# Attention and two mixture layers: K loaded in runs of 16s, a new order in the first columns, GpSimd sums in pieces

## The chip, the cores and the metric

The kernel runs on one core of one Trainium2 chip. The metric is the device time of one execution in microseconds (us). The kernel before has a median of 943.73 us over 3 runs (943.45 to 946.13).

## The reference

Three stages follow each other; all inputs are float32. The attention's queries are 8 batches x 8 heads x 576 rows x 64; K and V are averaged over 8 neighbouring rows first, so that each head has 72 keys.

```
k_p = k.reshape(B, H, Sp, pool, D).mean(axis=3)      # B,H,S,D = 8,8,576,64, pool = 8
v_p = v.reshape(B, H, Sp, pool, D).mean(axis=3)
scores = scale * np.matmul(q, k_p.transpose(0, 1, 3, 2))
attn = np.exp(scores - scores.max(-1)); attn /= attn.sum(-1) + 1e-09
x = np.matmul(attn, v_p)                              # then 4608 tokens x 512
# layer 1: e_idx = argmax(x @ w_gate + modality_bias[modality_id])
out[mask] = gate_w[mask, None] * (np.maximum(x[mask] @ w1[e], 0) @ w2[e])   # 8 experts, 512->1024->512
# layer 2: the same with its own weights for rows with x @ w_skip > 0; x is added, other rows stay x
```

## The kernel before

**Columns.** The attention works on 36 columns (c = 0 to 35) of 128 query rows, in a loop that runs three further turns (`LAG`), since the product with V lies three columns behind. In a column TensorE (PE) computes the scores S (L310, eight heads, keys from `KB`), transposes the queries of the column after next (qT, L289), transposes the exponentials of the column before (eT, L357), subtracts the row maxima from the scores (L336, "the exp matmul"; ScalarE's exponential follows it) and multiplies with V (AV, L377, for the column three back). VectorE (DVE) reduces the scores to their maxima `mx` (L316): the exp matmul waits for it. Each of these has few buffers: one PSUM tile for S, and one, `ps_m`, that everything occasional shares (transposed K and V, V times the gating weights, the counts R of the routing).

**K and V.** K and V come in as rows of 8 x 64 numbers (512 a row), and their sums over 8 are made on GpSimd (POOL) as a tree of three additions (L181, L182, L183), or on DVE as one reduction (L176). Batches 0 and 1 of K are loaded by batch (`kb`, `load_kb`, 126 rows at a time); batches 2 to 7 as four tiles of 108 rows (`kt`, `load_k`), each in two halves of four heads, one DMA a head. `prep_kb` and `prep_k` (L217 to L239) then transpose the sums on PE, `prep_v1` (L255) and `prep_v2` (L274) do it for V. The tables `pool_at` and `prep_at` say behind which column each of these stands.

**Loads.** All loads are issued by SyncE (SP) in one queue, in the order of `order` and as `next_kv` and `next_q` are called; eight DMA semaphores go round, so that SP's next issue waits for the one eight before.

**Routing beside the columns.** The first mixture layer needs every token's expert. Its work is cut into small steps of generators, of which `bg.tick()` takes the next; some five ticks fall in a column, twice as many from c = 22 (`bg.pace`). `route` (9 columns a call, started at c = 12, 21 and 30) takes the maximum of the gating values `LG` (`rt_mx`), marks the expert by three small GpSimd instructions (`rt_eq`, L840 to L844), reduces the marks (`rt_my`, L850, on DVE), makes a running count over the nine columns (a scan on DVE, L867, and the carry L871), ranks by two matmuls R (L882, L883), and leaves the position `BB`. `lag` gives the number of ticks between its steps. `route_places` then makes 18 tiles `OB` of 128x128 on GpSimd (L911), from which, after c = 30, a matmul W (L1031) and a gather fetch the first blocks of tokens. `count` makes a further R (L923) of the counts. In c = 32 and 33 `ps_x` transposes tokens of the first block, whose low half `xl` DVE writes (L320).

**After the attention** come the two layers in blocks of 256 tokens, where each float32 product is three matmuls. The change touches none of this.

Of the kernel before, what the change touches and what calls it, by code (L numbers as in the profile page):

```python
# [14 lines left out]
ALU = mybir.AluOpType  # L15
# [19 lines left out]


NB0 = 2
KT = (B - NB0) * SP // 4
TILES = [(NB0 * SP + KT * i, NB0 * SP + KT * i + KT) for i in range(4)]

KR = [(126 * i, min(126 * i + 126, H * SP)) for i in range(5)]
VC = 96
# [13 lines left out]
def attention(tc, g, q, k, v, mid, w_gate, bias, const, moe):  # L56
# [3 lines left out]
    nc = tc.nc  # L60
    with ExitStack() as ctx:
# [28 lines left out]
        cols = []  # L90
# [11 lines left out]
        raw_t = {}  # L102
# [5 lines left out]
        def load_kb(b, i0, i1):  # L108

            if ("kb", b) not in raw_t:  # L110
                raw_t["kb", b] = raw.tile([128, 5, POOL * D], F32, tag="k", name="kb", bufs=3)
            a = raw_t["kb", b]
            n = KR[i0][1] - KR[i0][0]
            for i in range(i0, i1):
                nc.sync.dma_start(out=a[0:n, i:i + 1, :], in_=rows(k, b, *KR[i], 1))

        def load_k(t, hf):
            a = raw.tile([128, 5, POOL * D], F32, tag="k", name="kt", bufs=3)[:, 0:4]
            for b, s0, s1, p0 in segments(t):
                for h in range(4):  # L120
                    nc.sync.dma_start(
                        out=a[p0:p0 + s1 - s0, h, :],
                        in_=k[b, 4 * hf + h, s0 * POOL:s1 * POOL, :].rearrange(
                            "(s r) d -> s (r d)", r=POOL),
                    )
# [58 lines left out]

        def sums_of(key, shape):
# [7 lines left out]
            pool_rows(d[0:n, i0:i1, :], raw_t["kb", b][0:n, i0:i1, :], eng)  # L193

        def pool_k(t, hf, eng):
            d = sums_of(("k", t), [KT, H, D])
            pool_rows(d[:, 4 * hf:4 * hf + 4, :], raw_t.pop(("k", t, hf))[0:KT], eng)

        def pool_v(b, hf, eng, i0=0, i1=3):
            d = sums_of(("v", b), [VC, 6, D])  # L200
# [222 lines left out]
        def idle():  # L423
            for _ in range(3):
# [2 lines left out]
        av_t = {}  # L427

        P, V = nc.gpsimd, nc.vector
        pool_at = {0: [(pool_kb, 1, 2, 4, P), (pool_kb, 1, 0, 2, V), (pool_kb, 1, 4, 5, V)],  # L430
                   1: [(pool_v, 1, 0, P)]}
# [5 lines left out]
        for b, cs in ((1, (3, 4, 4)), (2, (5, 6, 7)), (3, (10, 11, 12)), (4, (14, 15, 16)),  # L437
                      (5, (18, 19, 20)), (6, (20, 21, 22)), (7, (24, 25, 26))):
            for i, c in enumerate(cs):
                pool_at.setdefault(c, []).append((pool_v, b, 1, V, i, i + 1))  # L440
        prep_at = {1: [(prep_v1, 0)], 2: [(prep_kb, 1), (prep_v2, 0)],
                   5: [(prep_v1, 1)], 6: [(prep_v2, 1)], 7: [(prep_k, 0)],
                   8: [(prep_v1, 2, P)], 9: [(prep_v2, 2)], 11: [(prep_k, 1)],
                   13: [(prep_v1, 3, P)], 14: [(prep_v2, 3)],
                   17: [(prep_v1, 4)], 18: [(prep_v2, 4)], 20: [(prep_k, 2)],
                   21: [(prep_v1, 5)], 22: [(prep_v2, 5)], 24: [(prep_v1, 6)], 25: [(prep_k, 3)],
                   26: [(prep_v2, 6)], 28: [(prep_v1, 7)], 29: [(prep_v2, 7)]}

        def free_after(key):
# [110 lines left out]

        route_at = {12: (0, 9), 21: (9, 9), 30: (18, 9)}
        for c in range(NC + LAG):
            if c < NC:
                next_q(cols[c][0] + (5 if c > 1 else 4))
                next_kv(c)
                next_q(cols[c][0] + 5)
            bg.pace = {22: 2, 32: 1, 34: 2, 36: 3}.get(c, bg.pace)
            if 4 <= c < NC - 1:
                emit_S(c, lambda: emit_qT(c + 2))
            elif c < 4:  # L570
# [255 lines left out]
def route(tc, g, r, lg, mask, c0, n, sp, pp, eng, wait=1, then=(), lag=(0, 0)):  # L826
# [30 lines left out]
    if n > 2:  # L857
# [322 lines left out]
class Moe:  # L1180
# [307 lines left out]
    def prepare_first(self, c, sm, ps_q, ps_m, late):  # L1488
# [607 lines left out]
```

## Time and profile before

| | us |
|---|---|
| median of 3 runs | 943.73 |
| the profiled execution | 941.72 |
| its span in the trace | 940.0 |
| PE busy | 891.0 |
| DVE busy | 705.2 |
| GpSimd busy | 513.3 |
| ScalarE busy | 367.7 |

Busy times are of the whole span. The clock that TensorE was granted is on average 0.985 of full speed. The attention, to which the change belongs, ends a little after 200 us. A row of the timeline gives the start, the duration, the engine, the line, the operation, output and inputs, a count where equal instructions were merged, and in brackets the idle time of the engine before it and what released it.

### The profile page before, as it was taken

To read this page: it belongs to the slowest core of one execution; us is meant where nothing else is said; L and a number is where in the kernel's file an instruction comes from. 1 tells how busy PE (TensorE), PEld (TensorE's weight loads), DVE (VectorE), ACT (ScalarE), POOL (GpSimd) and SP (SyncE) were. 2 spreads that over 40 slices of the span, in tenths; PEclk is the share of its full clock that TensorE was granted. 3 is DMA by queue.
4 is the path that set the end of the run, shared out by engine and by line. 5 is a ranking of instruction groups with operands and counts; after the bars stand their busy time and mean duration, and the time that the engine had idled before them with its cause. 6 is when DMAs were issued, how large, how long until landed. Compare 5 with 4: busy or idle time off the path is not lost. (4 is left out here: it accounts for less than half of the span.)

```text
span 940.0 us, 19065 instructions
## 1 busy us (share of the span) xinstructions
PE 891.0 (95%) x6231; PEld 800.9 (85%) x6231; DVE 705.2 (75%) x1815; ACT 367.7 (39%) x727; POOL 513.3 (55%) x763
## 2 busy tenths in 40 slices
PE   8899989899999999998999979999989999999995
PEld 6799879888899999987999869999878988979993
DVE  5477786787778888889877898877565777688663
ACT  3466555453222222251222422213413556565551
POOL 6766696312246657665766557575554343445441
PEclk9899999999999999999999999999999999999999
DMA  9998975523212211431224421227114673671351
GB/s 235 222 254 250 263 206 157 185 70 113 69 65 86 74 41 55 152 144 66 85 81 135 167 79 64 75 81 246 62 61 149 207 236 128 202 246 37 111 161 44
DMA packets 86141, 126.07 MB, mean 134 GB/s; under 512 B 13192, under 2 KB 50104, under 8 KB 85866
## 3 DMA queue, kind: packets, MB, share of 16 engines
q1 hardware_dynamic: 75386, 96.68, 33.1%
q0 software_dynamic: 10608, 27.67, 9.7%
q8 instruction: 63, 1.03, 0.5%
q14 instruction: 84, 0.69, 0.2%
HBM read 182.09 MB, written 39.50 MB: 236 GB/s over the span
## 5 line engine op out<-in xcount | busy, mean ns | idle before, releaser
L1413 PE MATMUL ps_g<-xh,w1h 128*128 128x256 f32 x896 | 255.6, 285 | 3.9 <-DVE hl L1418 2.2
L1413 PE MATMUL ps_g<-xl,w1h 128*128 128x256 f32 x896 | 252.8, 282 | 2.2 <-DVE xl L1366 2.2
L1413 PE MATMUL ps_g<-xh,w1l 128*128 128x256 f32 x896 | 252.0, 281 | 0.0
L1743 DVE CUSTOM_DVE_ANT_0 hr<-x,W 128x512 bf16<-128x512 f32 x324 | 228.2, 704 | 19.1 <-DVEq L1342 6.3
L1462 PE MATMUL ps_g<-w2h,hh 128*128 128x512 f32 x464 | 189.8, 409 | 2.8 <-ACT w2h L1353 1.4
L1462 PE MATMUL ps_g<-w2h,hl 128*128 128x512 f32 x464 | 184.9, 399 | 7.2 <-DVE hl L1418 7.0
L1462 PE MATMUL ps_g<-w2l,hh 128*128 128x512 f32 x464 | 183.6, 396 | 0.0
L1413 PEld LDWEIGHTS ps_g<-xh,w1h 128*128 128x128 f32 x896 | 169.0, 189 | 9.0 <-DVE hl L1418 2.6
L1413 PEld LDWEIGHTS ps_g<-xl,w1h 128*128 128x128 f32 x896 | 168.4, 188 | 3.9 <-DVE xl L1366 3.0
L1413 PEld LDWEIGHTS ps_g<-xh,w1l 128*128 128x128 f32 x896 | 168.8, 188 | 0.0
L1417 ACT ACTIVATE hh<-ps_g 128x512 fp32r<-128x512 f32 (+1 forms) x116 | 67.6, 583 | 246.9 <-PE ps_g L1413 244.7
L1418 DVE SCALAR_TENSOR_TENSOR hl<-ps_g,hh 128x512 fp32r<-128x512 f32 (+1 forms) x116 | 77.5, 668 | 62.6 <-ACT hh L1417 39.0
L911 POOL TENSOR_SCALAR OB<-iota,BB,pay 128x128 bf16<-128x128 bf16 x126 | 110.8, 887 | 22.5 <-DVE BB L899 22.4
L1462 PEld LDWEIGHTS ps_g<-w2h,hl 128*128 128x128 f32 x464 | 87.6, 189 | 30.4 <-DVE hl L1418 8.7
L1462 PEld LDWEIGHTS ps_g<-w2h,hh 128*128 128x128 f32 x464 | 88.0, 190 | 22.2 <-issue 3.7
L1462 PEld LDWEIGHTS ps_g<-w2l,hh 128*128 128x128 f32 x464 | 88.1, 190 | 16.7
L1354 DVE TENSOR_TENSOR w2l<-w2r,w2h 128x512 fp32r<-128x512 f32 x112 | 75.3, 710 | 7.1 <-ACT w2h L1353 4.3
L1333 POOL TENSOR_TENSOR w1l<-w1r,w1h 128x512 fp32r<-128x512 f32 x36 | 46.6, 1314 | 60.6 <-ACT w1h L1330 60.4
L1709 POOL DMA_INDIRECT out_dram<-x,dsi x38 | 47.3, 1244 | 43.5 <-DMA out_dram<-x,dsi 14.8
L1353 ACT CAST w2h<-w2r 128x512 fp32r<-128x512 f32 x112 | 63.9, 617 | 1.4 <-ACTq L1973 1.4
L1330 ACT CAST w1h<-w1r 128x512 fp32r<-128x512 f32 x112 | 63.7, 620 | 0.5 <-ACT hh L1417 0.5
L1323 POOL DMA_INDIRECT xg<-xd,gidx x38 | 44.3, 1165 | 33.6 <-DVE rs_lo L1174 16.5
(298 smaller groups left out, 1403.9 us busy)
## 6 DMA issues: line engine op xcount, KB each, us to landing
w1r<-in_moe_w_dram SPq DMA_DIRECT2D x128, 512.0 KB
w2r<-in_moe_w_dram SPq DMA_DIRECT2D x124, 512.0 KB
x2s<-x SPq DMA_DIRECT2D x19, 522.0 KB
v<-in_v_dram SPq DMA_DIRECT2D x48, 192.0 KB
xd<-x SPq DMA_DIRECT2D x16, 520.0 KB
q_sb<-in_q_dram SPq DMA_DIRECT2D x16, 512.0 KB
kt<-in_k_dram SPq DMA_DIRECT2D x32, 144.0 KB
x2s<-OBx SPq DMA_DIRECT2D x16, 261.0 KB
```

The costliest lines, as they stand in the source:

```text
L911: e.tensor_scalar(g.ob(c)[:, i, :], g.iota, r.BB[:, c:c + 1], r.pay[:, i, c:c + 1], ALU.is_equal, ALU.mult)
L1323: self.nc.gpsimd.indirect_dma_start(out=self.xg[i % 2][:, t, 0:w], out_offset=None, in_=src, in_offset=bass.IndirectOffsetOnAxis(ap=gidx[: ...
L1330: self.nc.scalar.copy(self.w1h[f], raw)
L1333: low() if late is None else late.append(low)
L1353: self.nc.scalar.copy(self.w2h[f], raw)
L1354: (eng or self.nc.vector).tensor_tensor(self.w2l[f], raw, self.w2h[f].bitcast(F32), ALU.subtract)
L1413: nc.tensor.matmul(out, lhsT=a[f][:, k, :], rhs=b[:, k, :], start=(n == 0), stop=(n == 11))
L1417: nc.scalar.activation(out=hh, in_=whole, func=ACTF.Relu)
L1418: nc.vector.scalar_tensor_tensor(hl, in0=whole, scalar=0.0, in1=hh.bitcast(F32), op0=ALU.max, op1=ALU.subtract)
L1462: nc.tensor.matmul(ps, lhsT=a[f][:, tt], rhs=b[f], start=(n == 0), stop=(n == 23))
L1709: self.nc.gpsimd.indirect_dma_start(out=self.out, out_offset=bass.IndirectOffsetOnAxis(ap=self.dsi[i % 2][:, t:t + 1], axis=0), in_=self.x ...
L1743: self.nc.vector.tensor_tensor_reduce(out=self.junk, in0=self.x2[i % 2][:, t, 0:DM], in1=self.W9[:, e, :], scale=1.0, scalar=0.0, op0=ALU. ...
```

## The change

**K loads.** The four tiles of K have 120, 96, 120 and 96 rows in place of 108 each. A DMA takes four heads at once and its rows are a multiple of 16, with what is left over (8 rows) in a DMA of its own. The loads of batches 0 and 1 take 128, 128, 128, 128 and 80 rows (126 and 72 before; the surplus rows are not used).

**Pieces.** GpSimd's first additions are made one row group at a time (256 results each), the second two groups at a time; the third is as before. A half of a K tile has 7 instructions in place of 3, a half of V 6 in place of 3.

**First columns.** `prep_kb(1)` moves from the end of c = 2 to c = 3, behind the exp matmul of that column, so that column 3 stands ahead of it; `prep_v2(0)` moves ahead of the exp matmul of c = 2. Queries are split after that exponential, and the fifth reduction of the second K is one column later. Query loads are issued sooner than K and V.

**Later columns.** The V sums and preparations of batch 2 are a column later, and so is `prep_k(3)`, which now stands inside c = 26. In the routing the lags are other, the carry of the first two calls is made on GpSimd, one copy of the counts moves to ScalarE, the pace of the ticks changes a column earlier at the end, and a flag `bg.shut` holds the second R of `count` back until c = 35.

```
+KG = [NB0 * SP + n for n in (0, 120, 216, 336, 432)]
+TILES = [(KG[i], KG[i + 1]) for i in range(4)]
 def load_kb:
+                n = -(-(KR[i][1] - KR[i][0]) // 16) * 16
+                nc.sync.dma_start(out=a[0:n, i, :], in_=flat[r0:r0 + n])
 def load_k:
-                for h in range(4):
-                    nc.sync.dma_start(out=a[p0:p0 + s1 - s0, h, :], ...
+                cut = s0 + (s1 - s0) // 16 * 16
+                for x0, x1 in ((s0, cut), (cut, s1)):
+                    if x0 < x1:
+                        nc.sync.dma_start(out=a[p0 + x0 - s0:p0 + x1 - s0],
+                            in_=k[b, 4 * hf:4 * hf + 4, x0 * POOL:x1 * POOL, :].rearrange(
+                                "h (s r) d -> s h (r d)", r=POOL))
 def pool_rows:
-                eng.tensor_tensor(t1, a[:, :, 0:4 * D], a[:, :, 4 * D:], ALU.add)
-                eng.tensor_tensor(t2, t1[:, :, 0:2 * D], t1[:, :, 2 * D:], ALU.add)
+                for i in range(m):
+                    eng.tensor_tensor(t1[:, i], a[:, i, 0:4 * D], a[:, i, 4 * D:], ALU.add)
+                for i in range(0, m, 2):
+                    x = slice(i, min(i + 2, m))
+                    eng.tensor_tensor(t2[:, x], t1[:, x, 0:2 * D], t1[:, x, 2 * D:], ALU.add)
 the column loop:
+            if c == 0:
+                for n in (4, 5, 6):
+                    next_q(n)
+                    next_kv(0, 1)
+                next_kv(0)
...
+            elif c < NC:
+                next_q(cols[c][0] + (5 if c < 2 else 6))
+                next_kv(c)
-            bg.pace = {22: 2, 32: 1, 34: 2, 36: 3}.get(c, bg.pace)
+            bg.pace = {22: 2, 31: 1, 33: 2, 36: 3}.get(c, bg.pace)
+            elif c == 2:
+                emit_S(c)
+                emit_eT(c - 1)
+                prep_v2(0)
+                emit_exp(c)
+                split_q(2)
+            elif c == 3:
+                emit_S(c)
+                emit_eT(c - 1)
+                emit_qT(4)
+                emit_exp(c)
+                prep_kb(1)
+            if c == 26:
+                prep_k(3)
             emit_AV(c - LAG)
+            if c == 3:
+                emit_qT(5)
-        (nc.gpsimd, (5, 8) if c0 == 0 else (4, 12))
+        (nc.gpsimd, (5, 1) if c0 == 0 else (6, 3))
 def route:
-        V.tensor_copy(r.carry, I[:, :, n - 1])
+        eng.tensor_copy(r.carry, I[:, :, n - 1])
 def count:
-    nc.vector.tensor_copy(cb, r.carry)
+    (nc.scalar.copy if copy else nc.vector.tensor_copy)(cb, r.carry)
+    while g.bg.shut:
+        yield
 def prepare_first, at c = 32 and 33:
+            self.g.bg.shut = True
```

**The first columns on PE.** Before, from the transposed queries of column 4 (`ps_q`) to the scores of column 4 (the `ps_s<-KB_129` in the last row), with the rest of the nine `ps_k` instructions of the second K left out:

```order
L289 MATMUL ps_q<-ident,qs 128x128 x4
L217 MATMUL ps_k<-ident,kb 64x126
...
L222 MATMUL ps_k<-ident,kb 64x72
L274 MATMUL ps_g<-WGV,vt 96x32 x3
L310 MATMUL ps_s<-KB_128,qt 128x144 x4
L357 MATMUL ps_et<-ident,ec 96x128 x6
L336 MATMUL ps_s<-mx,nident 128x288 x2
L289 MATMUL ps_q<-ident,qs 128x128 x4
L377 MATMUL ps_av<-VB_134,et 128x146 x6
L310 MATMUL ps_s<-KB_129,qt 128x144 x4
```

The same place now, from V times the gating weights (`ps_g`) to the scores of column 4:

```order
L282 MATMUL ps_g<-WGV,vt 96x32 x3
L344 MATMUL ps_s<-mx,nident 128x288 x2
L318 MATMUL ps_s<-KB_128,qt 128x144 x4
L365 MATMUL ps_et<-ident,ec 96x128 x6
L297 MATMUL ps_q<-ident,qs 128x128 x4
L344 MATMUL ps_s<-mx,nident 128x288 x2
L225 MATMUL ps_k<-ident,kb 64x126
...
L230 MATMUL ps_k<-ident,kb 64x72
L385 MATMUL ps_av<-VB_134,et 128x146 x6
L297 MATMUL ps_q<-ident,qs 128x128 x4
L318 MATMUL ps_s<-KB_129,qt 128x144 x4
```

The scores of column 3 (`KB_128`), their exp matmul and `ps_g` stand ahead of the second K's transposes now.

**GpSimd between c = 16 and c = 23.** Before, from the end of the second half of the third K tile, with the 18 tiles `OB` and two halves of V between it and the marks `rt_eq` of the second routing:

```order
L183 TENSOR_TENSOR k<-t_1466 108x256
L911 TENSOR_SCALAR OB<-iota,BB_664,pay_666 128x128 x2
L181 TENSOR_TENSOR t_1536<-v 96x768
L182 TENSOR_TENSOR t_1537<-t_1536 96x384
L183 TENSOR_TENSOR v<-t_1537 96x192
L911 TENSOR_SCALAR OB<-iota,BB_664,pay_666 128x128 x8
L181 TENSOR_TENSOR t_1673<-v 96x768
L182 TENSOR_TENSOR t_1674<-t_1673 96x384
L183 TENSOR_TENSOR v<-t_1674 96x192
L911 TENSOR_SCALAR OB<-iota,BB_664,pay_666 128x128 x8
L840 TENSOR_TENSOR rt_eq<-LG,rt_mx 128x72
```

Now, from the end of the first half of that tile; the two halves of V follow as before behind the last row here, in pieces, with eight and three `OB` behind them, and then `rt_eq`:

```order
L191 TENSOR_TENSOR k<-t_1408 120x256
L944 TENSOR_SCALAR OB<-iota,BB_663,pay_665 128x128 x3
L187 TENSOR_TENSOR t_1479<-kt 120x256 x4
L190 TENSOR_TENSOR t_1480<-t_1479 120x256 x2
L191 TENSOR_TENSOR k<-t_1480 120x256
L944 TENSOR_SCALAR OB<-iota,BB_663,pay_665 128x128 x4
L187 TENSOR_TENSOR t_1551<-v 96x256 x3
```

The first `OB` stands a half of a K tile earlier, so that this half now lies between the first `OB` and `rt_eq`.

**DVE in c = 22 and 23.** Before, from the V scaling `VB` of c = 22 to the reduced marks `rt_my` of c = 23 (each `mx` begins a column):

```order
L316 TENSOR_REDUCE mx<-ps_s 128x8
L260 TENSOR_TENSOR VB_139<-v,half 96x12x64
L176 TENSOR_REDUCE v<-v 96x64
L406 TENSOR_REDUCE LG<-lg 128x8
L838 TENSOR_REDUCE rt_mx<-LG 128x9
L395 TENSOR_SCALAR rec<-ps_av 128x8
L397 RECIPROCAL rec<-rec 128x8
L399 TENSOR_TENSOR lg<-ps_av,rec 128x64
L402 TENSOR_TENSOR x<-ps_av,rec 128x512
L316 TENSOR_REDUCE mx<-ps_s 128x8
L276 TENSOR_TENSOR VB_139<-ps_g,half 96x12x8
L176 TENSOR_REDUCE v<-v 96x64
```

(the next row there is `rt_my`). Now, the end of c = 22 and the `mx` of c = 23:

```order
L181 TENSOR_REDUCE v<-v 96x64
L871 TENSOR_REDUCE rt_mx<-LG 128x9
L414 TENSOR_REDUCE LG<-lg 128x8
L883 TENSOR_REDUCE rt_my<-rt_eq 128x9
L403 TENSOR_SCALAR rec<-ps_av 128x8
L405 RECIPROCAL rec<-rec 128x8
L407 TENSOR_TENSOR lg<-ps_av,rec 128x64
L410 TENSOR_TENSOR x<-ps_av,rec 128x512
L324 TENSOR_REDUCE mx<-ps_s 128x8
```

`rt_my` stands one column earlier, two rows behind `rt_mx`, and ahead of the `mx` of column 23.

## Rows read from the trace of the kernel before

**Rows 1.** The page: busy time and share of the span of each engine.
```profile
PE 891.0 (95%) x6231; PEld 800.9 (85%) x6231; DVE 705.2 (75%) x1815; ACT 367.7 (39%) x727; POOL 513.3 (55%) x763
```

**Rows 2.** Windows: length, busy us (instructions) of each engine, clock, DMA share, GB/s.
```profile
20.00:30.00 10.00, 6.61 (x40) 4.40 (x37) 3.75 (x4) 5.08 (x9) 8.92 (x11) 0.88 1.03 242
30.00:40.00 10.00, 9.16 (x60) 8.72 (x61) 3.42 (x8) 3.77 (x10) 5.58 (x6) 0.78 0.85 220
...
100.00:110.00 10.00, 10.00 (x76) 9.98 (x75) 6.79 (x20) 5.57 (x12) 4.96 (x6) 0.86 1.09 302
...
180.00:190.00 10.00, 9.28 (x70) 8.93 (x71) 5.60 (x20) 4.15 (x12) 3.88 (x6) 0.83 0.49 186
```

**Rows 3.** Timeline of PE in columns 1 to 4.
```profile
20.90 0.39 PE L255 MATMUL ps_v<-ident,v 96*128 96x96 f32 x2 [0.58 <-POOL v L183]
...
23.79 0.51 PE L336 MATMUL ps_s<-mx,nident 128*128 128x288 f32 x2 [0.84 <-DVE mx L316]
25.74 0.66 PE L289 MATMUL ps_q<-ident,qs 128*128 128x128 f32 x4 [1.44 <-ACT qs L167]
...
30.84 1.17 PE L274 MATMUL ps_g<-WGV,vt 128*96 128x32 f32 x6 [1.37 <-ACT KB L231]
31.82 2.27 PE L310 MATMUL ps_s<-KB,qt 128*128 128x144 f32 x8
...
37.23 1.15 PE L310 MATMUL ps_s<-KB,qt 128*128 128x144 f32 x8
```

**Rows 4.** Timeline of ACT: the split of the queries of columns 4 and 5.
```profile
24.64 1.04 ACT L167 COPY qs<-q_sb 128x1024 f32<-128x1024 f32 x1 [3.69 <-DMA q_sb<-in_q_dram]
```

**Rows 5.** Timeline of POOL: the first addition of the first K tile, batch 2.
```profile
34.91 2.35 POOL L181 TENSOR_TENSOR t<-kt 108x1024 f32<-108x1024 f32 x1 [4.11 <-DMA kt<-in_k_dram]
```

**Rows 6.** Timeline of PE: the transposes of that K tile, before S(8).
```profile
54.49 0.53 PE L239 MATMUL ps_k<-ident,k 108*128 108x108 f32 x4
```

**Rows 7.** Timeline of PE: the later waits, c = 17 to 34.
```profile
97.79 0.51 PE L336 MATMUL ps_s<-mx,nident 128*128 128x288 f32 x2 [1.92 <-DVE mx L316]
...
130.21 0.51 PE L336 MATMUL ps_s<-mx,nident 128*128 128x288 f32 x2 [1.15 <-DVE mx L316]
...
135.46 0.51 PE L336 MATMUL ps_s<-mx,nident 128*128 128x288 f32 x2 [0.84 <-DVE mx L316]
...
139.28 0.40 PE L239 MATMUL ps_k<-ident,k 108*128 108x108 f32 x2 [1.62 <-POOL k L183]
...
162.62 1.04 PE L1031 MATMUL W<-er_oa,OB 128*128 128x2 bf16 x36
...
170.82 0.51 PE L336 MATMUL ps_s<-mx,nident 128*128 128x288 f32 x2 [0.98 <-DVE mx L316]
...
180.72 0.18 PE L923 MATMUL R<-rc_cb,ones 128*128 128x8 bf16 x1 [2.19 <-DVE xl L320]
```

**Rows 8.** Timeline of DVE: two scans, the reduced marks, the low half of `ps_x`.
```profile
92.33 2.37 DVE L867 TENSOR_TENSOR_SCAN rt_i<-within,rt_ms 128x72 bf16<-128x72 f32 x1
...
127.91 0.23 DVE L850 TENSOR_REDUCE rt_my<-rt_eq 128x9 f32<-128x72 f32 x1 [1.86 <-POOL rt_eq L844]
...
168.43 0.31 DVE L867 TENSOR_TENSOR_SCAN rt_i<-within,rt_ms 128x72 bf16<-128x72 f32 x1
...
175.57 0.68 DVE L320 TENSOR_TENSOR xl<-ps_x,xh 128x512 fp32r<-128x512 f32 x1
```

**Rows 9.** GpSimd's additions of K by form, 0 to 170 us.
```profile
L181 POOL TENSOR_TENSOR t<-kt 108x1024 f32<-108x1024 f32 x8 | 18.9, 2357 | 4.3 <-DMA kt<-in_k_dram 4.1
...
L183 POOL TENSOR_TENSOR k<-t 108x256 f32<-108x256 f32 x8 | 5.9, 741 | 0.6
```

**Rows 10.** Timeline of POOL: from the first `OB` to the marks, and a K half.
```profile
104.89 1.59 POOL L911 TENSOR_SCALAR OB<-iota,BB,pay 128x128 bf16<-128x128 bf16 x2 [8.20 <-DVE BB L899]
...
126.66 0.30 POOL L840 TENSOR_TENSOR rt_eq<-LG,rt_mx 128x72 f32<-128x72 f32 x1
...
136.54 1.87 POOL L182 TENSOR_TENSOR t<-t 108x512 f32<-108x512 f32 x1
```

More of the change, by code (lines that the diff above doesn't have):

```diff
@@ L37 @@
 NB0 = 2
-KT = (B - NB0) * SP // 4
-TILES = [(NB0 * SP + KT * i, NB0 * SP + KT * i + KT) for i in range(4)]
+KG = [NB0 * SP + n for n in (0, 120, 216, 336, 432)]
+TILES = [(KG[i], KG[i + 1]) for i in range(4)]
+KN = [KG[i + 1] - KG[i] for i in range(4)]
 KR = [(126 * i, min(126 * i + 126, H * SP)) for i in range(5)]
@@ L112, in load_kb @@
             a = raw_t["kb", b]
-            n = KR[i0][1] - KR[i0][0]
+            flat = k.rearrange("b h (s r) d -> (b h s) (r d)", r=POOL)
             for i in range(i0, i1):
-                nc.sync.dma_start(out=a[0:n, i:i + 1, :], in_=rows(k, b, *KR[i], 1))
+                n = -(-(KR[i][1] - KR[i][0]) // 16) * 16
+                r0 = b * H * SP + KR[i][0]
+                nc.sync.dma_start(out=a[0:n, i, :], in_=flat[r0:r0 + n])
         def load_k(t, hf):
@@ L119, in load_k @@
             for b, s0, s1, p0 in segments(t):
-                for h in range(4):
[L121 to L125, printed above, removed]
+                cut = s0 + (s1 - s0) // 16 * 16
+                for x0, x1 in ((s0, cut), (cut, s1)):
+                    if x0 < x1:
+                        nc.sync.dma_start(
+                            out=a[p0 + x0 - s0:p0 + x1 - s0],
+                            in_=k[b, 4 * hf:4 * hf + 4, x0 * POOL:x1 * POOL, :].rearrange(
+                                "h (s r) d -> s h (r d)", r=POOL),
+                        )
             raw_t["k", t, hf] = a
@@ L195, in pool_k @@
         def pool_k(t, hf, eng):
-            d = sums_of(("k", t), [KT, H, D])
-            pool_rows(d[:, 4 * hf:4 * hf + 4, :], raw_t.pop(("k", t, hf))[0:KT], eng)
+            d = sums_of(("k", t), [128, H, D])[0:KN[t]]
+            pool_rows(d[:, 4 * hf:4 * hf + 4, :], raw_t.pop(("k", t, hf))[0:KN[t]], eng)
         def pool_v(b, hf, eng, i0=0, i1=3):
@@ L234, in prep_k @@
             bg.settle()
-            n = KT
-            ks = sum_t.pop(("k", t))
+            n = KN[t]
+            ks = sum_t.pop(("k", t))[0:n]
             ps = ps_m.tile([128, 4, 128], F32, tag="m", name="ps_k")
@@ L429, in attention @@
         P, V = nc.gpsimd, nc.vector
-        pool_at = {0: [(pool_kb, 1, 2, 4, P), (pool_kb, 1, 0, 2, V), (pool_kb, 1, 4, 5, V)],
-                   1: [(pool_v, 1, 0, P)]}
+        pool_at = {0: [(pool_kb, 1, 2, 4, P), (pool_kb, 1, 0, 2, V)],
+                   1: [(pool_v, 1, 0, P), (pool_kb, 1, 4, 5, V)]}
         for t, c0 in enumerate((3, 8, 16, 23)):
@@ L436, in attention @@
             pool_at.setdefault(c0, []).append((pool_v, b, 0, P))
-        for b, cs in ((1, (3, 4, 4)), (2, (5, 6, 7)), (3, (10, 11, 12)), (4, (14, 15, 16)),
+        for b, cs in ((1, (3, 4, 4)), (2, (6, 7, 8)), (3, (10, 11, 12)), (4, (14, 15, 16)),
                       (5, (18, 19, 20)), (6, (20, 21, 22)), (7, (24, 25, 26))):
@@ L440, in attention @@
                 pool_at.setdefault(c, []).append((pool_v, b, 1, V, i, i + 1))
-        prep_at = {1: [(prep_v1, 0)], 2: [(prep_kb, 1), (prep_v2, 0)],
+        prep_at = {1: [(prep_v1, 0)],
                    5: [(prep_v1, 1)], 6: [(prep_v2, 1)], 7: [(prep_k, 0)],
-                   8: [(prep_v1, 2, P)], 9: [(prep_v2, 2)], 11: [(prep_k, 1)],
+                   9: [(prep_v1, 2, P)], 10: [(prep_v2, 2)], 11: [(prep_k, 1)],
                    13: [(prep_v1, 3, P)], 14: [(prep_v2, 3)],
                    17: [(prep_v1, 4)], 18: [(prep_v2, 4)], 20: [(prep_k, 2)],
-                   21: [(prep_v1, 5)], 22: [(prep_v2, 5)], 24: [(prep_v1, 6)], 25: [(prep_k, 3)],
+                   21: [(prep_v1, 5)], 22: [(prep_v2, 5)], 24: [(prep_v1, 6)],
                    26: [(prep_v2, 6)], 28: [(prep_v1, 7)], 29: [(prep_v2, 7)]}
@@ L562, in attention @@
         for c in range(NC + LAG):
-            if c < NC:
-                next_q(cols[c][0] + (5 if c > 1 else 4))
-                next_kv(c)
-                next_q(cols[c][0] + 5)
-            bg.pace = {22: 2, 32: 1, 34: 2, 36: 3}.get(c, bg.pace)
+            if c == 0:
[4 more added lines that the diff above has]
+            elif c == 2:
+                next_kv(c)
+                next_q(7)
+            elif c < NC:
+                next_q(cols[c][0] + (5 if c < 2 else 6))
+                next_kv(c)
+            bg.pace = {22: 2, 31: 1, 33: 2, 36: 3}.get(c, bg.pace)
+            if c == 35:
+                bg.shut = False
             if 4 <= c < NC - 1:
                 emit_S(c, lambda: emit_qT(c + 2))
-            elif c < 4:
+            elif c < 2:
                 if c > 0:
@@ L575, in attention @@
                 emit_qT(c + 2)
+            elif c == 2:
+                emit_S(c)
[9 more added lines that the diff above has]
+                prep_kb(1)
             elif c == NC - 1:
@@ L597, in attention @@
                 moe.open_third()
-            ahead = c + (3 if c < 2 else 4)
-            if ahead < NC and cols[ahead][0] not in qs_t:
+            ahead = c + 4
+            if ahead < NC and c > 2 and cols[ahead][0] not in qs_t:
                 split_q(cols[ahead][0])
@@ L621, in attention @@
                 c0, n = route_at[c]
-                eng, lag = (nc.vector, (0, 0)) if c0 == 18 else (nc.gpsimd, (5, 8) if c0 == 0 else (4, 12))
+                eng, lag = (nc.vector, (0, 0)) if c0 == 18 else (nc.gpsimd, (5, 1) if c0 == 0 else (6, 3))
                 bg.add(route(tc, g, g.r1, g.LG[:, c0:c0 + n, :], None, c0, n, sm, ps_m, eng, 1,
@@ L671, in __init__ @@
         self.q = []
-        self.hold = False
+        self.hold = self.shut = False
         self.pace = 1
```

## The prediction

> **What bounds the kernel now.** I read the page first: PE is busy for 95% of the span [rows 1], so a change can save only what PE waits and what it runs at the low clock. The list of PE's waits by what ended them comes next; the reader is to see that nearly all of it in the attention is the exp matmul waiting for DVE's maxima and a few single waits for a buffer or for GpSimd. The timeline of PE then gives each wait its column [rows 3, 7], and the windows what follows it [rows 2]: in 100 to 110 us, behind the 1.92 us wait at 97.79, PE is busy for 10.00 us at a granted clock of 0.86. [...] In 180 to 190, behind the 2.19 us wait, it is 0.83: 3.4 us, 1.7 us lost. The waits of 1.15 and 0.98 us had none behind them. I price a wait of 1.6 us or more at its length plus 1.6 us. The timelines of DVE and GpSimd then say who was late [rows 8, 10].
>
> **The change part by part.**
>
> *First columns.* Before, PE waits 0.58 us for V's sums, 0.84 for maxima, 1.44 for the split queries and 1.37 for the copies of the second K [rows 3]: 4.23 us. The clock falls too: 0.88 in 20 to 30 us and 0.78 in 30 to 40 [rows 2], that is 2.4 and 4.4 us at the low level, of which the 1.37 us are idle, so 5.4 us of work ran at half speed and 2.7 us were lost. The scores of column 3 show it: 2.27 us against 1.15 for those of column 4. After, `ps_g` stands ahead of the second K and no longer waits for its copies; S(3) and its company fill the time in which queries and sums of the second K arrive; that K's copies then have AV(0) and qT(5) to cover them. ScalarE no longer holds the exponential of column 2 behind the copy that waits 3.69 us for queries until 24.64 [rows 4]; the transposes of column 4 come at about 26, after that copy's end (24.64 + 1.04 = 25.7). V's first piece can start on one of its three loads. One wait is new: S(3) stands right behind the exp matmul of column 2 and needs the tile that ScalarE's exponential reads. From that engine's 1.04 us for 1024 elements [rows 4] its 576 take an estimated 0.6. Sum: 4.2 + 2.7 - 0.6 = 6.3 us, S(4) at about 31 in place of 37.23. The ends: 7.5 if the new wait hides, 0 if the loads come so much later that PE waits as long.
>
> *Loads.* In 20 to 40 us the DMA engines are busy for 1.03 and 0.85 of the time at 242 and 220 GB/s [rows 2]: they move what they can, so larger DMAs change when a K half lands by little. I take nothing; the ends are one microsecond either way on the first K tile, which hides while PE doesn't wait for it. [...]
>
> *Pieces.* GpSimd's additions take 2357 ns for 1024 elements a partition and 741 for 256 [rows 9]: 2.1 ns an element and 0.2 us an instruction. A K half of 7 pieces takes 7 x 0.74 = 5.2 us in place of 4.4 (1792 elements and 3 starts), a V half with three starts more 0.6 us more. For a piece I take 0.74; the ends are 0.6 (less start cost back to back) and 1.0 (stretched beside DVE).
>
> What pieces can bring back is on DVE: the scan took 2.37 us beside a 2.36 us addition, 0.31 when GpSimd stood idle [rows 8]. But the scan of the first two routings, and the carry, now run while GpSimd itself waits for the carry, with no addition beside them; so the 1.92 us at 97.79 and the 0.84 at 135.46 go with either part of the change. [...]
>
> *Columns 15 to 30.* Removed: the waits of 1.92, 1.15, 0.84 and 1.62 us [rows 7], and two stretches at the low clock, behind the first and the last: 5.5 + 3.2 = 8.7 us. The 1.62 at `prep_k(3)` goes because both halves of that tile start right behind the carry and the transposes come later.
>
> But GpSimd's queue becomes the bound of c = 22. Before, it goes from the first `OB` at 104.89 to `rt_eq` at 126.66 [rows 10], 21.8 us, and the three marks let DVE's `rt_my` go at 127.91, after a wait of 1.86 [rows 8]: 23.0 us in all, where DVE would have asked after 21.2. Now the second half of the third K tile lies in that stretch too (the order shows it between the third and the fourth `OB`): 5.2 us more, and two V halves in pieces 1.2 more: 29.4. DVE asks at c = 22 rather than 23, having got `BB` at c = 17 rather than 18: again five columns, with the long V scaling of c = 22 ahead of it in its column, about 22 us. It waits 7.4. Queued behind `rt_my` on DVE are the divisions of the product with V and the maxima of column 23, and for these the exp matmul waits. Before, 1.86 on DVE became 1.15 on PE, so PE takes 0.7 less: 6.7 us, and 1.6 for the clock: 8.3. Sum of this part: 8.7 - 8.3 = 0.4 us gained. The ends are 8.7 (no wait) and -4 (pieces of 1.0: 19 pieces x 0.26 = 4.9 us more on GpSimd).
>
> *Columns 30 to 35.* The 0.98 us at 170.82 go with the matmul R that now comes a column later. The R that waited 2.19 for `xl` [rows 7] is held back behind the first product of the layer; in its stead the rank's R now stands in c = 33 between the two `ps_x`, in the same single buffer, and waits for the `xl` of the first. From the end of the scores DVE has the maxima, a weight's low half and `xl`, each at least the 0.68 of [rows 8], 2.0 us, and PE only the transposes of 0.66 [rows 3]: a wait of 1.4. Saved: 0.98 + 0.8 = 1.8 us, with the low clock kept. Ends 0 and 4.8 (no wait, no low clock).
>
> What is behind c = 35 keeps its instructions; I cost it at nothing, since the layers are PE's own work and weights were loaded at half the DMA's capacity (0.49 [rows 2]).
>
> **Sum.** 6.3 + 0.4 + 1.8 = 8.5 us from the profiled execution's 941.72: 933.2. That execution lies 2.0 under the median of 943.73, so on the median 935.2.
>
> **The rivals.**
>
> *GpSimd keeps up.* The `rt_my` wait stays under 1 us. For it: pieces could cost less than 0.74, and `OB` less than the 0.8 each that the row at 104.89 shows (1.59 for two) [rows 10]. Against: 18 `OB` stand ahead of the marks in one queue, and even pieces of 0.6 take only 19 x 0.14 = 2.7 us off. Then the columns 15 to 30 give up to 8.7: 941.7 - 16.8 = 924.9, on the median 926.9; half of it is 931.
>
> *The first K tile comes too late.* Before, its first half is there at 34.91 [rows 5], its sums need two halves of 4.4 us, and PE asks at 54.49 [rows 6]: some 10 us to spare. Now PE asks 6.3 us sooner, at 48.2; ahead of the second half SP issues 256 and 512 KB of queries and a tenth more rows, about 1 MB or 4.2 us at 231 GB/s, the mean of the two windows, and each half's sums are 0.8 us longer. A second half that before had landed by 39.3 at the latest (34.91 + 4.4) lands by 43.5 and is summed by 48.7: nothing to spare. Two to four microseconds later PE waits at the end of c = 7 and loses 1.6 more by the clock: the sum falls to 4.9 or 2.9, on the median 939 to 941.
>
> *Slower: the pieces are stretched.* An addition of 512 elements took 1.87 us at 136.54 [rows 10], 0.6 more than by the formula, while DVE worked in the same memory. With more than twice the starts more of them can meet DVE. Between the first `OB` and `rt_eq` stand 19 pieces, and 20 more between the second carry and the `OB` that W (162.62 before [rows 7]) needs. At 0.3 us each that is 11.7 us in a chain on which PE waits twice: 8.5 - 11.7 = 3.2 us slower, 946.9; the sign turns at 0.22 us a piece. For it is that one row; against it, the eight additions of 1024 elements have a mean of 2357 ns [rows 9], the length of the one at 34.91 [rows 5], so that such a stretch is rare.
>
> **How the numbers follow.** Forecast 0.5 (its own range 931 to 939), GpSimd keeps up 0.15, late K tile 0.22, stretched pieces 0.10, anything else 0.03. A measurement of this kernel tells about 0.3%, 2.8 us, from no change: 940.9 and 946.6. The forecast and the first rival are faster, and half of the second: 0.74. The other half and the edge of the forecast are within: 0.14. The stretched pieces and a little: 0.12. The range from 927 to 943 leaves out half of the first rival and nearly all of the third.
>
> **What would show it.** S(4) on PE near 31, no PE wait over 1 us before it, and a clock near 1.00 in 20 to 40; `prep_k(0)` without a wait for GpSimd (else the second rival). The scan of c = 15 at about 0.3 us. `rt_my` of c = 22 with an idle time of 6 to 8 us behind `rt_eq`, and the exp matmul of c = 23 with some 6.7, then a low clock: without them the step on GpSimd's queue is wrong. Pieces of 256 at 0.74 us. R in c = 33 with 1.4 us. The prediction is wrong as a whole if the time from the end of the attention to the end of the span changes by more than a microsecond.

## The result and the profile after

The changed kernel takes 958.34 us (median of 4 runs, 956.41 to 959.03) against 943.59 for the kernel before beside it (also 4): a ratio of 1.0143 (95% interval 1.012 to 1.0165), 1.4% slower. The forecast was 935.2, faster. Its profiled execution took 958.02 us, with a span of 956.3; the mean granted clock is 0.971, against 0.985.

The reader should first compare where a column's scores S(c) begin on PE, read from the timelines of both kernels (us):

```
            S(4)   S(7)   S(9)  S(17)  S(22)  S(24)  S(27)  S(35)  first ps_x after it    end of span
before     37.23  50.12  59.74  93.26 118.58 126.83 145.79 184.94       217.38              940.0
after      31.05  47.00  60.70  95.92 119.02 136.08 154.73 190.93       228.40              956.3
after-bef. -6.2   -3.1   +1.0   +2.7   +0.4   +9.3   +8.9   +6.0        +11.0               +16.3
```

The lead of 6.2 us is there at column 4 and gone at column 9; nine are lost between columns 22 and 24, and five between S(35) and the first transposes (`ps_x`) of the second block. PE's timeline of the changed kernel shows the waits (the columns of a row are as in [rows 3]):

```profile
24.11 1.25 PE L318 MATMUL ps_s<-KB,qt 128*128 128x144 f32 x8 [0.79 <-ACT ec L348]
...
31.05 1.15 PE L318 MATMUL ps_s<-KB,qt 128*128 128x144 f32 x8
...
45.27 0.70 PE L282 MATMUL ps_g<-WGV,vt 128*96 128x32 f32 x6 [1.25 <-ACT vt L267]
47.00 1.25 PE L318 MATMUL ps_s<-KB,qt 128*128 128x144 f32 x8 [1.03 <-ACT ec L348]
...
53.54 0.42 PE L247 MATMUL ps_k<-ident,k 120*128 120x120 f32 x2 [0.59 <-POOL k L191]
...
60.70 1.25 PE L318 MATMUL ps_s<-KB,qt 128*128 128x144 f32 x8 [2.61 <-ACT ec L348]
...
125.29 0.85 PE L344 MATMUL ps_s<-mx,nident 128*128 128x288 f32 x2 [4.00 <-DVE mx L324]
...
150.41 0.63 PE L344 MATMUL ps_s<-mx,nident 128*128 128x288 f32 x2 [3.57 <-DVE mx L324]
...
183.98 0.21 PE L915 MATMUL R<-M,trim 128*128 128x72 bf16 x1 [1.61 <-DVE xl L328]
...
212.32 1.58 PE L1066 MATMUL W<-er_oa,OB 128*128 128x2 bf16 x54 [3.15 <-DVE er_oa L1051]
```

The first two rows answer to [rows 3]: the waits of 1.44 and 1.37 us are gone. The next waits name ScalarE, and ScalarE's timeline says what held it there: the split of the queries, in order ahead of the exponentials.

```profile
43.88 1.04 ACT L172 COPY qs<-q_sb 128x1024 f32<-128x1024 f32 x1 [3.61 <-DMA q_sb<-in_q_dram]
...
56.40 1.05 ACT L172 COPY qs<-q_sb 128x1024 f32<-128x1024 f32 x1 [3.60 <-DMA q_sb<-in_q_dram]
```

The first addition of the K tile, which answers to [rows 5], comes 4.8 us later than before, not sooner; GpSimd's timeline:

```profile
39.69 2.78 POOL L187 TENSOR_TENSOR t<-kt 120x256 f32<-120x256 f32 x4 [9.32 <-DMA kt<-in_k_dram]
```

DVE's timeline has the scan of the first routing, the wait for V in front of the maxima of column 22, and the marks, which answer to [rows 8]:

```profile
91.13 0.29 DVE L900 TENSOR_TENSOR_SCAN rt_i<-within,rt_ms 128x72 bf16<-128x72 f32 x1
...
122.20 1.02 DVE L181 TENSOR_REDUCE v<-v 96x64 f32<-96x512 f32 x1 [4.38 <-DMA v<-in_v_dram]
...
130.26 0.23 DVE L883 TENSOR_REDUCE rt_my<-rt_eq 128x9 f32<-128x72 f32 x1 [2.71 <-POOL rt_eq L877]
```

Most of these waits go back to data that had not landed: queries at 43.88 and 56.40, K at 39.69, V at 122.20. The 3.57 us at c = 26 and the 3.15 in front of W have other causes (below). The windows, as in [rows 2], show the engines that bring them, and the clock behind the waits:

```profile
30.00:40.00 10.00, 9.36 (x79) 8.95 (x77) 7.09 (x16) 5.82 (x13) 0.68 (x2) 1.00 1.14 187
...
50.00:60.00 10.00, 7.50 (x60) 6.70 (x58) 5.53 (x13) 5.18 (x12) 9.71 (x34) 0.92 1.11 200
120.00:130.00 10.00, 6.00 (x33) 5.75 (x32) 5.29 (x11) 2.71 (x8) 9.75 (x15) 0.67 1.05 245
210.00:220.00 10.00, 6.83 (x78) 6.61 (x77) 4.71 (x15) 3.48 (x10) 0.37 (x1) 0.66 0.25 80
```

The DMA share adds up the times of the packets, as a share of the 16 engines' time, so the 1.14 of 30 to 40 us says that times of packets overlap. It is higher there than before (1.14 against 0.85) and less is moved (187 against 220 GB/s); the low clock of that window is gone (1.00 against 0.78). The low clock is now in 120 to 130 and 210 to 220, among others (60 to 70 and 130 to 140 are at 0.83 and 0.82).

### The profile page after: what moved, and what is told of

It reads as the page before. It is cut to its first block, busy times and chain, and to the rows that moved or that the text cites. A ratio compares the mean times of both kernels' runs of the same rounds, so it can differ in the third digit from the quotient of the medians.

```text
span 956.3 us, 19058 instructions
## 1 busy us (share of the span) xinstructions
PE 899.8 (94%) x6231; PEld 810.9 (85%) x6231; DVE 701.5 (73%) x1810; ACT 368.3 (39%) x730; POOL 518.9 (54%) x822
## 3 DMA queue, kind: packets, MB, share of 16 engines
q8 instruction: 63, 1.03, 0.5%
## 5 line engine op out<-in xcount | busy, mean ns | idle before, releaser
L1497 PE MATMUL ps_g<-w2h,hh 128*128 128x512 f32 x464 | 192.2, 414 | 3.1 <-ACT w2h L1388 2.0
L944 POOL TENSOR_SCALAR OB<-iota,BB,pay 128x128 bf16<-128x128 bf16 x126 | 108.5, 869 | 15.1 <-DVE BB L932 15.0
L385 PE MATMUL ps_av<-VB,et 96*128 96x146 f32 (+1 forms) x480 | 64.1, 299 | 0.0
```

The source lines that it names most:

```text
L385: nc.tensor.matmul(ps[p0:p1, j // 3, o:o + 2 * VW], lhsT=t[:, j, p0:p1], rhs=VB[b % NR][:, j].rearrange("p i w -> p (i w)"), start=(j % 3 ...
L944: e.tensor_scalar(g.ob(c)[:, i, :], g.iota, r.BB[:, c:c + 1], r.pay[:, i, c:c + 1], ALU.is_equal, ALU.mult)
L1497: nc.tensor.matmul(ps, lhsT=a[f][:, tt], rhs=b[f], start=(n == 0), stop=(n == 23))
```

## The experiments

Two theories went in. The loads theory: the DMA engines bound the kernel until about 130 us, and the four-head DMAs make it worse. The routing theory: GpSimd's queue and the new lags cost the time. A third part came out of the profiles, the late count: the flag that holds `count` back, with the pace that changes a column earlier. Ratios are to the kernel before, measured beside each version on the same chip. Versions are compared by them, since the median of the kernel before itself was between 943.58 and 946.82 on the chips used.

**One head a DMA again, in the changed kernel.**

```
-   ... in_=k[b, 4 * hf:4 * hf + 4, x0 * POOL:x1 * POOL, :] ...   # cut at multiples of 16
+   for h in range(4): ... in_=k[b, 4 * hf + h, s0 * POOL:s1 * POOL, :] ...
```

> The changed kernel (958.3 us) with one edit undone: the K tiles are again loaded one head a DMA, whole segments of 72, 48, 24 rows; tile sizes, pieces, column order and routing stay. Loads theory (the DMA engines bound the kernel until 130 us, and the four-head DMAs move fewer bytes for the same busy time): K, queries and V land 3 to 5 us sooner, the waits of ScalarE for queries at 43.9 and 56.4 and of DVE for V at 122.2 shrink to under 1.5 us, 941 to 948 us. Routing theory (the GpSimd queue and the new lags cost the time at c = 22 and 26): 955 to 959 us, the waits for loads as they are.

956.8 us, 1.014 (1.010 to 1.0179). The time hardly moves, and neither expectation fits whole. The first K half is summed from 35.67, ScalarE's two waits for queries shrink to 0.32 and 2.80 us, and S(9) is at 55.68, five microseconds sooner than with four heads, S(17) at 89.71. The lead lasts until column 22, where DVE waits 7.18 us for V (117.93) and PE 5.42. Most of the gain went into a longer wait for the next load. The profiled execution, at 952.82 well under the median, is still 2.6 us ahead of the changed kernel's at S(35) (188.30).

**The old order of loads, in the changed kernel** (the `next_q` and `next_kv` calls of before).

> The changed kernel with the old order of loads on SyncE (queries of later columns not ahead of K and V). Loads theory, in the form that order and not shape is to blame (1024 packets of 256 bytes of queries stand ahead of the first K tile): the first K half lands at 35 to 36 in place of 39.7 and the sums end before PE asks, 948 to 953 us; if the shape of the K loads is to blame, the waits move from K to queries and the time stays at 956 to 962. Routing theory: 956 to 960.

963.24 us, 1.0211 (1.0166 to 1.0256). Worse, a little above the 956 to 962 expected if the shape is to blame. The first K half is summed from 37.78, 1.9 us sooner, but PE itself waits 4.62 us for queries at 45.92, and S(9) is at 63.67. By that row the new start needs its queries early; that they are asked for early is not the fault.

**Old lags and carries, in the changed kernel.**

```
-   (nc.gpsimd, (5, 1) if c0 == 0 else (6, 3))
+   (nc.gpsimd, (5, 8) if c0 == 0 else (4, 12))       # and carry, rc_cb on DVE
```

> The changed kernel with the routing's old lags and its carries and the copy of the counts back on DVE (the pace, the late count and the fourth K tile's place stay new). Routing theory: the first OB again stand behind both halves of the third K tile, the wait of DVE for the reduced marks at c = 22 and the crowd of short DVE instructions in c = 25 go, 944 to 950 us. Loads theory: DVE still waits for V at c = 21 (4 us) and the stretch behind keeps its low clock; 953 to 958 us.

953.33 us, 1.0093 (1.0062 to 1.0125), at the lower edge of what the loads theory expected. The wait for the marks is gone, that for V is not (4.70 us at 124.42), and the 3.57 of c = 26 become 0.82 and 1.83.

**Whole sums, in the changed kernel.**

> The changed kernel with GpSimd's sums whole again (3 instructions a half). Both theories: each K half 0.8 us and each V half 0.5 us shorter on GpSimd, but one addition of 2.4 us can hold a DVE instruction. If GpSimd's queue is what PE waits for (routing theory), 2 to 4 us off the changed kernel, 953 to 956; if loads are (loads theory), no change outside 957 to 960.

959.53 us, 1.0149 (1.010 to 1.0198): no change that can be told, so the pieces are not the cause of the loss. The profile does differ: S(9) is at 57.33, and then PE waits 3.18 us for maxima at 68.61.

**The new start alone, in the kernel before.**

> The kernel before with the new order of columns 1 to 3 alone (column 3 ahead of the second K, queries split later); loads, sums, routing as before. Prediction's step: S(4) at about 31 in place of 37.2, and the 6 us stay: 937 to 939 us against 944. Loads theory: S(4) at 31, but K, queries and V land when they did, so PE waits for them by c = 9 to 22 and half or all of the 6 us are gone: 941 to 946 us.

945.49 us, 0.9985 (0.9964 to 1.0006). The loads theory's own test: S(4) is at 32.51, and S(9) at 59.74 and S(10) at 64.14, where they were before (that it is to the hundredth is chance). ScalarE's timeline of this kernel shows the landings that set this:

```profile
46.47 1.04 ACT L167 COPY qs<-q_sb 128x1024 f32<-128x1024 f32 x1 [4.71 <-DMA q_sb<-in_q_dram]
...
55.51 1.05 ACT L167 COPY qs<-q_sb 128x1024 f32<-128x1024 f32 x1 [2.02 <-DMA q_sb<-in_q_dram]
```

In the kernel before, the same two copies ran at 47.00 and 55.52. PE comes sooner, the second load comes when it came.

**The late count alone, in the kernel before.**

```
+            if c == 35: bg.shut = False
-            bg.pace = {22: 2, 32: 1, 34: 2, 36: 3}
+            bg.pace = {22: 2, 31: 1, 33: 2, 36: 3}
+            self.g.bg.shut = True        # c = 32, 33; count yields while it is set
```

> The kernel before with the new pace from c = 31 and the late count (shut until c = 35) alone. Prediction's step: the 2.19 us of R become 1.4, 1 to 2 us faster, 942 to 943 us. Rival (the second W waits for its operand, as in all profiles of the changed kernel: 3.15 us at 212 and a granted clock of 0.66 in 210 to 220): 3 to 6 us slower, 947 to 950.

948.18 us, 1.0015 (0.9995 to 1.0034). The interval, worked out, is 0.5 us faster to 3.2 slower: it leaves out a gain of 1 to 2 us and most of a loss of 3 to 6. The profile has a gain and a loss, and on PE's timeline they lie 28 us apart (this view ends at 205 us, inside W, and so counts 43 of W's 54 matmuls):

```profile
175.55 0.21 PE L884 MATMUL R<-M,trim 128*128 128x72 bf16 x1 [1.62 <-DVE xl L320]
...
203.88 1.28 PE L1035 MATMUL W<-er_oa,OB 128*128 128x2 bf16 x43 [3.14 <-DVE er_oa L1020]
```

S(35) is 2.4 us sooner (182.50), but the second W, which waited for nothing at 201.55 before, stands 3.14 us. The count feeds, one tick a step, the chain of short DVE instructions that ends in W's operand `er_oa`; held back, it pushes them past the place where PE wants it.

**Without the late count, in the changed kernel.**

> The changed kernel with the old pace from c = 32 and without the late count. Rival of b_tail: W's wait of 3.15 us goes, 4 to 6 us off the changed kernel, 952 to 955. Prediction's step: the R of c = 34 waits 2.2 again and the time is 1 to 2 us longer than the changed kernel, 959 to 961.

956.55 us, 1.0104 (1.0074 to 1.0135). W's wait is gone, the 2.19 of R is back. By the ratios that is 0.4% less loss than the changed kernel's 1.0143, some 3.7 us, but the two intervals overlap; it is near the 4 to 6 us that the rival expected, and not clear of the scatter.

**Four parts undone together** (one head a DMA, old lags, old count, the fourth K tile's place).

> The changed kernel with four parts undone together: K tiles one head a DMA, old lags and carries, old pace and count, the fourth K tile's transposes back at the end of c = 25. What stays is the start, the pieces, the order of loads, the tile sizes and the runs of 128 rows of the first two K. If the parts found so far make up the loss, the sum of (loads 4 to 10 us, lags 5, tail 5) brings 940 to 946; a time over 950 says that what stays costs too.

946.7 us, 1.001 (0.9988 to 1.0032): the loss is gone. What stays of the change holds a lead of 5.3 us at S(22) (113.30), and then DVE waits for V:

```profile
117.05 1.02 DVE L179 TENSOR_REDUCE v<-v 96x64 f32<-96x512 f32 x1 [4.94 <-DMA v<-in_v_dram]
```

**Four-head loads alone, in the kernel before** (the change's `load_k` on the old tiles).

> The kernel before with the K tiles (still 108 rows) loaded four heads a DMA, cut at multiples of 16 rows (64 and 8, 32 and 4); all else as before. Loads theory: the four-head DMAs alone make what lands after them late; ScalarE's wait for queries before c = 8 grows from 1.3 to over 3 us, S(9) comes 2 to 5 us later than 59.7, and the kernel is 2 to 6 us slower, 948 to 952 against 946. Rival (the shape is harmless, and it was the early queries that delayed K): S(9) within 1 us of 59.7, the time within 2 us.

950.63 us, 1.0073 (1.0052 to 1.0094): slower by 7 us by itself, and S(9) at 66.01, 6.3 us late. The DMA view of 20 to 60 us shows why; here its packets and bytes in the kernel before:

```profile
DMA packets 9242, 9.14 MB, mean 228 GB/s; under 512 B 1725, under 2 KB 6180, under 8 KB 9236
...
q1 hardware_dynamic: 9236, 9.07, 91.5%
```

and with this one edit:

```profile
DMA packets 8225, 8.12 MB, mean 203 GB/s; under 512 B 1482, under 2 KB 5410, under 8 KB 8221
...
q1 hardware_dynamic: 8221, 8.07, 106.9%
```

The packets' times add up to 107% of the engines' span in place of 92%, and a ninth less is moved.

**Four heads a DMA, but whole segments, in the changed kernel** (no DMA of 8 rows).

> The changed kernel with four heads a DMA, but whole segments (72, 48, 24 rows) and no DMA of 8 rows. If the small DMAs of 8 rows are what slows the loads, S(9) comes back to the 55.7 of the kernel with one head a DMA; if four runs a row in one DMA are, it stays at 60 to 61.

954.96 us, 1.0125 (1.0096 to 1.0154); S(9) at 57.99, between the two answers. The same stretch in the DMA view of this kernel, and then of the changed one:

```profile
DMA packets 9253, 8.85 MB, mean 221 GB/s; under 512 B 1434, under 2 KB 6363, under 8 KB 9248
...
q1 hardware_dynamic: 9248, 8.80, 102.4%
```

```profile
DMA packets 9022, 8.31 MB, mean 208 GB/s; under 512 B 1474, under 2 KB 6335, under 8 KB 9017
...
q1 hardware_dynamic: 9017, 8.25, 110.7%
```

How the delay divides between the cut and the four heads these numbers can't tell. The version with whole sums loads just as the changed kernel does, and has 8.84 MB at 111% and S(9) at 57.33; with one head a DMA and the new start, S(9) lies between 53.54 and 57.27 and the bytes between 8.63 and 9.50 MB, from one version to the next. What holds in every profile is the share: 90 to 97% with one head a DMA, 102% here, 107 to 111% with the cut. What in the engines takes the time is not settled.

**V of batch 6 later, with one head a DMA, old lags and count**; the fourth K tile as in the change. Then **the same with whole sums**.

```
-   (6, (20, 21, 22))
+   (6, (22, 22, 23))
```

> The version with one-head DMAs, old lags, pace and count, plus two edits: DVE's sums of V of batch 6 one to two columns later (after c = 22, 22, 23 in place of 20, 21, 22), and the fourth K tile's transposes in c = 26 as in the change. Loads theory: the wait of 4.9 us for V at 117 and its low clock go, PE keeps the 5 us it leads at c = 22, 938 to 942 us against 946. Rival: the lead meets the next load (queries or K of batch 6 and 7) within a few columns and the time stays at 944 to 947.

> The same with GpSimd's sums whole again. If pieces are neutral it equals the version with pieces within 2 us; if they cost (0.8 us a K half, 0.5 a V half on a queue that DVE waits for at c = 23), it is 1 to 3 us faster; if they spare DVE (a scan or carry held by a 2.4 us addition at c = 16), 2 to 3 us slower.

941.71 us, 0.9987 (0.9967 to 1.0008), and 944.59, 1.0027 (0.9999 to 1.0055). By the ratios neither differs clearly from the kernel before; the 941.71 lies in the range expected, but beside a kernel before of 943.58 and not 946. The wait for V is gone, S(24) is at 119.45, 7.4 us ahead of before, and the next wait takes its place, GpSimd's marks:

```profile
125.16 0.23 DVE L881 TENSOR_REDUCE rt_my<-rt_eq 128x9 f32<-128x72 f32 x1 [5.53 <-POOL rt_eq L875]
```

With whole sums it is 4.28; pieces and whole sums can't be told apart in time, since the intervals meet.

**The same V edit under the new lags and count, one head a DMA.**

> The changed kernel (new lags, pace and count) with K tiles one head a DMA and DVE's sums of V of batch 6 after c = 22, 22, 23. Prediction's step, now that V is there in time: DVE waits 6 to 8 us for the marks at c = 22, PE 5 to 7 us, and the low clock follows. Rival (GpSimd keeps up, and the 1.2 to 2.7 us seen so far are its own): under 3 us. In both the 3.6 us at c = 26 and W's 3.1 us stay, 948 to 955 us against 944.

954.97 us, 1.0095 (1.0067 to 1.0122). Against the version with V later (0.9987), which differs from it by the old lags, carries, pace and count alone, this gives the price of the routing's edits and the late count together: 1.1% or some 10 us, with intervals far apart. It also measures the forecast's own term. First DVE, then PE, in this kernel's timeline:

```profile
123.09 0.23 DVE L881 TENSOR_REDUCE rt_my<-rt_eq 128x9 f32<-128x72 f32 x1 [8.29 <-POOL rt_eq L875]
```

```profile
125.21 0.85 PE L342 MATMUL ps_s<-mx,nident 128*128 128x288 f32 x2 [6.93 <-DVE mx L322]
```

**Nine of the 18 `OB` tiles on DVE, in the version with V later**; then **with whole sums**.

```
-   nc.vector if c0 == 18 else None
+   nc.vector if c0 in (0, 18) else None
```

> The version with V of batch 6 later (old lags, 941.7 us), and nine of the first routing's 18 OB tiles made on DVE, as the third routing does. Theory: GpSimd's queue from the first OB to the marks is 7 us shorter, the 5.5 us that DVE waits at c = 23 fall under 1, PE's 5.8 us and the low clock go; the lead of 7 us stays to c = 35 but for the 1.7 us at the fourth K tile: 934 to 938 us against 944. Rival: nine tiles of 0.3 us make DVE late (maxima of c = 18 to 22 later), or the lead meets a further load; 939 to 943.

> The same with GpSimd's sums whole. Pieces cost GpSimd 0.8 us a K half and 0.6 a V half, which no longer matters when its queue has room: within 1.5 us of the version with pieces. If whole additions hold DVE (scan and carry of c = 16 at 2.4 and 1.2 us, two maxima late): 2 to 3 us slower than it.

941.62 us, 0.9953 (0.9929 to 0.9978), and 943.73, 0.9969 (0.9953 to 0.9985): both faster than the kernel before, the first by 0.5%, less than expected. The marks are waited for 2.45 us rather than 5.53, S(25) is at 125.90 against 132.31. But at c = 25 and 26 DVE is late again (PE waits 1.96 and 1.82 us, 135 to 138), and S(35) is only 2.5 us ahead. The lead meets one wait after the other.

Taken together: the four-head loads cost 0.7% by themselves, the routing's edits and the late count 1.1%, and with these undone (and the fourth K tile back in its place) the loss is gone. The prices can't be added one by one, since a lead won at one place meets the next wait.

## Why the prediction was wrong

**The start, 6.3 us: the mechanism right, the gain not kept.** S(4) came at 31.05 ("about 31"), the new wait for the exponential was 0.79 (0.6 forecast), the clock in 20 to 40 us went to 1.00. The step that failed is what the sum did with it: "S(4) at about 31 in place of 37.23" was carried to the end as 6.3 us, though the term's own lower end, "0 if the loads come so much later that PE waits as long", described what happened. The kernel with the start alone shows that the loads need not even come later: the copy of its second queries starts at 55.51, as before at 55.52, both times behind a wait for them, so that there PE's waits in the first columns were no cost of their own. That is no bound for good: with queries asked for sooner, one head a DMA, V later and the old lags and count, S(9) is at 53.87 and the lead grows to 7.4 us at S(24).

**Loads: costed at nothing, with ends of one microsecond; measured at about 7.** I read the share of 1.03 as proof that the shape doesn't matter. It showed that packets were under way all the time; it said nothing about how many bytes they move: in 20 to 60 us 9.14 MB at 91.5% in the kernel before, 8.12 at 106.9% with four heads a DMA. In the changed kernel the first K half is summed 4.8 us later, with one head a DMA 0.8 us later (35.67); four heads a DMA alone make it 3.5 us later in the kernel before (38.38) and that kernel 7 us slower. In the changed kernel the same edit undone gave back no time that can be told (1.014 against 1.0143): what it gained by S(9) met the wait for V.

Of the 128 rows in the first two K loads no gain is shown: in the first 25 us the changed kernel moved 6.08 MB against 5.92, but the kernels with 126 rows have 5.65 to 6.16 and those with 128 rows 5.99 to 6.32. For the tiles, whose row counts in multiples of 16 came together with four runs a row and DMAs of 8 or 4 rows, less was moved: 8.12 against 9.14 MB in the 40 us shown.

**The second rival, the late K tile, was the nearest**, but priced at 2 to 4 us and one wait for K. The measured loss from S(4) to S(9) is 7.1 us, most of it waits for queries through ScalarE, which the rival did not name; for the K sums PE waits 0.59 us. Which of the two is late varies: with the same loads and start, PE waits 2.51 us for the K sums in the version with old lags and 3.06 in the one without the late count, and S(9) is at 60.5 in both.

**GpSimd's queue at c = 22: right, and hidden.** The forecast was 7.4 us on DVE and 6.7 on PE. In the changed kernel DVE waits 4.38 for V and then only 2.71 for the marks, since it was late already; with V there in time it is 8.29 and 6.93. The landing of V at 122 was not in the forecast at all: in the kernel before, the sum of the same piece of V ended by 118.4 with no wait.

**Columns 15 to 30, removed waits: right in part.** The scan takes 0.29 us and the clock in 100 to 110 is 1.00, as said. The 1.92 us at c = 17 became 1.48 with another cause, DVE waiting 1.64 us for a store of `x` to leave its buffer. The 1.62 of the fourth K tile is gone, but 3.57 us come at c = 26, from the chain of short DVE instructions that the new lags and the pace of two put into c = 25. (The lower end of this part, -4, should have been -4.5 by its own figures, 0.4 less 4.9.) The 1.6 us that the sum takes for the clock behind a long wait is an estimate from the kernel before: behind its waits of 1.92, 1.62 and 2.19 us the clock was 0.86, 0.83 and 0.83 in 100 to 110, 140 to 150 and 180 to 190, which is 1.4 to 1.7 us lost, and in the middle of the low stretch 0.50 (100 to 102, 141 to 143, 182 to 184), so that the 3.4 us of the prediction are the time at half speed. In the changed kernel the price was not fixed: behind the wait of 4.00 us the clock was 0.50 in 125 to 130 and 0.64 in 130 to 135, some 4 us lost, and behind the 1.61 of R it was 1.00 in 180 to 190, nothing lost.

**The late count: R right (1.4 forecast, 1.61 measured), what it pushes not seen.** I costed "what is behind c = 35" at nothing; W's 3.15 us and the clock of 0.66 behind it lie there. From S(35) to the first `ps_x` behind it the changed kernel takes 5.0 us more. The prediction's own sign of being wrong as a whole, more than a microsecond behind the attention, is met. W stands 3.13 to 3.16 us in all eight profiles with the late count, and in none without it.

**Pieces: right.** A piece takes 0.70 us (2.78 for four, 0.74 forecast), and the slower rival, stretched pieces, did not happen: from 0 to 170 us the pieces of the first additions have means of 722 to 770 ns.

Still open: behind that first `ps_x` the changed kernel takes 727.9 us and the profiled execution of before 722.6. The seven versions with the old lags and count, and with no edit behind the attention, take 724.6 to 727.8 (V later: 726.1; start alone: 727.0), so that the execution of before lies 2.0 below all of them and that of the changed kernel 0.1 above. How much of the 5.3 us belongs to the change is open; the cause was not looked for.

## What to carry to other kernels

Ask of every wait that goes which engine is full beside it. Where the next load lands when it landed before, a faster start only moves the wait to that landing (the second copy of queries started at 55.51 with the new start and at 55.52 before), so the price of such a stage is read from its landings, not from its compute's idle time; what it gains is kept only as far as every later load and every helper engine is ready for it. And a share of 1 is no licence to reshape the DMAs: compare the share and the bytes moved in a fixed stretch, in more than one profile, since here the higher share moved less (8.12 MB at 106.9% against 9.14 at 91.5%) and the bytes varied between versions with the same K loads and start (8.63 to 9.50 MB). A step that is held back moves everything that its queue of ticks feeds: here W, which then waited 3.14 us.

## What the runs showed of the hardware

A chain of short DVE instructions on few elements ran slowly while GpSimd worked through pieces: in the changed kernel, with GpSimd in additions of 96x256 from 145.17 to 148.43, DVE's timeline shows

```profile
145.18 0.74 DVE L928 CAST rt_ri<-rt_ra 128x9 int32<-128x9 f32 x1
145.96 0.65 DVE L930 TENSOR_SCALAR rt_ri<-rt_ri 128x9 int32<-128x9 int32 x1
146.65 0.65 DVE L932 CAST BB<-rt_ri 128x9 f32<-128x9 int32 x1
147.33 0.65 DVE L934 TENSOR_TENSOR RH<-rt_ra,BB 128x9 f32<-128x9 f32 x1
147.89 0.63 DVE L1042 TENSOR_TENSOR er_am<-M,star 128x144 f32<-128x144 bf16 x1
```

where in the version with `OB` on DVE the same cast and the next row took 0.17 us each, at 137.65 and 137.86, as GpSimd's last addition (137.09 to 137.67) ended. Each of the five lasts about as long as one piece (0.70), as if it were held once for each piece; by that, cutting GpSimd's work small did not spare this chain of short instructions. The copy of the carry shows the same with pieces and whole sums: with V later it took 0.51 us (129.22) and ended with a piece of GpSimd's, with whole sums 1.17 (128.78) and ended with an addition of 1.26, each to 0.03 us. Why these instructions last so long beside GpSimd's no run here shows.
